# First f and decay rows issued by ScalarE, raw loads of three pairs queued ahead, first k rounded by GpSimd, first probabilities turned in float32

## The chip, the cores and the metric

The kernel runs on one core of one Trainium2 chip. The metric is the device time of one execution in microseconds (us). TensorE (PE in the profile, PEld for its weight loads), VectorE (DVE), ScalarE (ACT), GpSimd (POOL) and SyncE (SP, which here only issues DMAs) run side by side, each through its own queue in order.

## The reference

Causal attention with a decay, then a mixture of experts with one expert per token. Cut to what matters here:

```python
scores = scale * q @ k.T                       # 8 batches x 8 heads, 576 x 64
cum    = cumsum(log(clip(f, 1e-4, 1)), -1)     # f: one number per token and head
scores = where(causal, -1e9, scores + cum[..., :, None] - cum[..., None, :])
attn   = exp(scores - rowmax); attn /= attn.sum(-1) + 1e-9
x      = attn @ v                              # then the experts: gate, w1, relu, w2
```

## The kernel before

Heads go in pairs: 32 pairs n, each on 128 partitions with one head in 64 of them. The program is one stream over steps (n, i), i from 0 to 6, in `attention_all`. In step (n, i) the scores of pair n are made (`s_steps`), the probabilities of pair n-1 are turned (transposed) on TensorE (`t_steps`), and in i = 1 the product with v of pair n-2 is made (`av`, L540). Routing and the experts' work are mixed into the later pairs and follow them. At the end of each step `order.pin()` (L807) keeps what was traced on each engine in program order; all SP DMAs go through `sp_dma` (L215) in program order too.

**Scores.** A score tile is a sum of two products in float32r (`smm`, L408): the first of `qk1` (q rounded in 64 partitions, what rounding left in the other 64) with the rounded k, the second of `Q2s`/`K2s`, 68 partitions that hold the raw q and k's remainder in 64 partitions and, in rows 64 to 67, the decay: cumulated log f of queries and keys and constants. `Q2s` and `K2s` exist twice, so pair n+2 writes where pair n was read. Score tiles go to three PSUM buffers (`ps_s`); VectorE adds the mask and takes the row extreme (`s_red`, L420), ScalarE takes the exponential (`s_exp`, L426).

**Operands of a pair.** `load_pair` (L219) loads a pair's raw q (two halves h, 320 KB each) and k (288 KB each); raw buffers are for three pairs. For pair 0: `first_q` (L344, ScalarE rounds q, then copies raw q into `Q2s`), `first_k` (L352, ScalarE rounds k, head by head), `second_q` (L357) and `second_k` (L360), remainders on VectorE (`lo`, L329). For pair 1 the same in the steps of pair 0, with the copy into `Q2s` on GpSimd. From pair 2 on GpSimd does `q_parts` (L367) and `copies` (L376), and k is rounded by `k_first` (L372; ScalarE for pair 2, VectorE later).

**The start.** SP issues the load of f (L241), pair 0 and pair 1's q. VectorE clips f, ScalarE takes the log (two table loads around it), VectorE scans and splits it in two (L249 to L263). SP then issues the decay rows of pair 0 (`c_rows`, L391: five small DMAs from the tile `xT0w` into `Q2s`/`K2s`; j is the head), pair 1's k, pair 2's q, rows of pair 1, pair 2's k. In step (1, 0) follow the rows of pair 2, pair 3's four loads and `c_writes` (L717: the rows of all later pairs to DRAM, 608 KB), in (1, 2) pair 4's loads, in (2, 0) `load_c` for pair 3 (L383: rows back from DRAM). `load_v` loads pair n's v in step (n, 3). GpSimd makes constant rows, masks and identities at the start.

**Turning.** `turn` (L475) transposes a 128x128 block with the float32r identity, reading the probabilities under a float32r name (`c.words`; `c.values` is the same memory named float32). A pair has 25 such blocks. The copies out of PSUM are VectorE's for pair 0 (`e` in `t_steps`) and mostly ScalarE's later.

Of the kernel before, what the change touches and what calls it, by code (L numbers as in the profile page):

```python
# [19 lines left out]
P = 128  # L20
# [147 lines left out]
def setup_consts(c, tc):  # L168
    c.ident = c.const.tile([P, P], F32, name="ident")
    make_identity(tc.nc, c.ident)  # L170
    c.identr = c.const.tile([P, P], F32R, name="identr")
    tc.nc.gpsimd.tensor_copy(c.identr, c.ident)


def attention_all(c, tc, qkT, va, vb, f, wgd, x_dram, batch_done, more_consts, extra):
# [15 lines left out]
    with ExitStack() as st:  # L191
# [27 lines left out]
        def load_pair(n, parts=(0, 1)):  # L219
# [21 lines left out]
        sp_dma(fr, f)  # L241
        warm = c.const.tile([1, 1], F32, name="warm")
        V.memset(warm, 1.0)
        tc.keep_in_program_order(nc.scalar.activation(warm, warm, AF.Ln))
        load_pair(0)
        load_pair(1, (0,))
        V.memset(ones, 1.0)
        V.memset(cum[:, 512:], 0.0)
        V.tensor_scalar(fr, fr, 1.0e-4, 1.0, ALU.max, ALU.min)  # L249
        nc.scalar.activation(fr, fr, AF.Ln)  # L250

# [28 lines left out]


        mask = ap_.tile([P, 512], F32, name="mask")
        nc.gpsimd.memset(mask, 0.0)
        nc.gpsimd.affine_select(
            mask[:, 384:], mask[:, 384:], [[-1, P]], ALU.is_ge, NEG,
            base=0, channel_multiplier=1,
        )
        maskj = ap_.tile([P, JW], F32, name="maskj")
        nc.gpsimd.memset(maskj, 0.0)
        for j in range(2):  # L290
            mj = maskj[j * 64 : j * 64 + 64, JW - 64 :]
            nc.gpsimd.affine_select(
                mj, mj, [[-1, 64]], ALU.is_ge, NEG, base=0, channel_multiplier=1
            )
        setup_consts(c, tc)
        const_rows(1)


# [3 lines left out]
        def late_consts():  # L302
            nc.gpsimd.memset(wg, 0.0)
            nc.gpsimd.memset(gTs[1][:, S - 512 :], 0.0)
            for i in range(2):
                nc.gpsimd.memset(c.values[i, "J"][:, S:], 0.0)
            c.more = more_consts()
# [10 lines left out]
        for vb_t in vbs:  # L318
            nc.gpsimd.memset(vb_t[64:KB], 0.0)
# [22 lines left out]
        pin = tc.keep_in_program_order  # L342

        def first_q(n):  # L344
            qk1, raw, q2 = operands(n), raws[n], Q2s[n]
            pin(nc.scalar.copy(qk1[:, 0:QW], raw[:, 0:QW]))
            if n == 0:
                pin(nc.scalar.copy(q2[0:64], raw[0:64, 0:QW]))
            else:
                nc.gpsimd.tensor_copy(q2[0:64], raw[0:64, 0:QW])  # L350

        def first_k(n):  # L352
            qk1, raw = ops[n][0], raws[n]
            for c0, c1 in ((QW, QW + S), (QW + S, QW + 2 * S)):
                pin(nc.scalar.copy(qk1[:, c0:c1], raw[:, c0:c1]))  # L355

        def second_q(n):  # L357
            pin(lo(V, n, ops[n][0][64:128, 0:QW], 64, 0, QW))

        def second_k(n):  # L360
            k2 = ops[n][3]
            for j in range(2):
                lo(V, n, k2[0:64, j], 0, QW + j * S, QW + (j + 1) * S)
# [27 lines left out]
        def c_rows(n, j):  # L391
# [3 lines left out]
            if j == 0:  # L395
                sp_dma(k2c[:, 0, :], r[:, :, 0:S])
                sp_dma(q2c[:, 0:640], r)
            else:
                sp_dma(k2c[:, 1, 0:512], r[:, :, 0:512])
                sp_dma(k2c[:, 1, 512:], r[:, :, S:640])  # L400
                sp_dma(q2c[:, 640:], r)
# [6 lines left out]
        def smm(out, n, parts, k0, kw):  # L408

            q1, k1, q2, k2 = ops[n]  # L410
            i, last = 0, 2 * len(parts) - 1
            for ql, kl in ((q1, k1), (q2, k2)):
# [18 lines left out]

        def s_tiles(n, items):

            b, p = divmod(n, NPAIR)
            pb = psum(ps_s)
            o = 0
            for j, t in items:
                w = P * (t + 1)
                smm(pb[:, o : o + w], n, [(j, j * 640 + P * t)], 0, w)
# [35 lines left out]
        def turn(out, words):  # L475

            note(nc.tensor.transpose(out.bitcast(F32R), words, c.identr))  # L477

        def t_tiles(n, items, engs):
# [3 lines left out]
            for j, t in items:  # L483
                for k in range(t + 1):
                    turn(pt[:, o : o + P], region(c.words, n, j, t)[:, P * k : P * k + P])
# [11 lines left out]
        def t_one(n, eng):  # L497
            aT = aTs[n]
            pt = psum(ps_t)
            for j in range(2):  # L500
                for k in range(2):
                    o = P * (2 * j + k)
                    turn(pt[:, o : o + P], region(c.words, n, j, 1)[:, P * k : P * k + P])
# [5 lines left out]
        def t_joint(n, eng):  # L509
            aT, sc = aTs[n], region(c.words, n, 0, -1)  # L510
# [11 lines left out]
        def t_last(n, pt):  # L522

            turn(pt[0:KB], region(c.words, n, 0, -1)[:, 512 : 512 + KB])
# [155 lines left out]
        def s_steps(n):  # L680
# [3 lines left out]
                      [(0, 1), (1, 1)])  # L684
            r = [(lambda g=g: (s_begin(n) if n not in nms else None, s_tiles(n, g)),
# [1072 lines left out]
```

## Time and profile before

| what | value |
|---|---|
| median of 3 runs (lowest to highest) | 797.3 us (797.06 to 799.41) |
| profiled execution, its own time | 800.95 us |
| its span, first to last instruction | 799.2 us |
| busy: PE | 773.7 us (97%) |
| busy: ACT, DVE, POOL | 513.3, 579.9, 541.7 us |
| mean granted TensorE clock | 0.993 |
| DMA | 114.70 MB, 144 GB/s over the span |

A span's start is the first instruction; times in the rows count from there. The profiled execution took 3.65 us more than the median of the runs. The busy share of PE includes the time in which a matmul runs at the lower clock, so it doesn't show by itself where time can be won.

### The profile page before, as it was taken

Reading aid. Unit: us, or ns where it says so; the run is one execution under the profiler, and the core shown is the slowest. Engines: PE = TensorE matmul, PEld = TensorE weight load, DVE = VectorE, ACT = ScalarE, POOL = GpSimd, SP = SyncE. Lnnn points to the kernel's source line nnn. Section 1 sums busy time; section 2 is a strip of 40 time slices with the busy share of each in tenths; the row PEclk is TensorE's granted clock in tenths of the full one; section 3 lists DMA queues with packets and bytes.
Section 4 is the critical chain, followed back from the end, with each engine's and each line's share of the span. In section 5 each row is a group of like instructions: output and inputs, shape, how many; then the busy total and the mean of one; then the engine's idle time right before and its main releaser. Section 6 shows DMA issues by size and latency. Waiting matters only on the chain.

```text
span 799.2 us, 16185 instructions
## 1 busy us (share of the span) xinstructions
PE 773.7 (97%) x5496; PEld 673.7 (84%) x5496; DVE 579.9 (73%) x1654; ACT 513.3 (64%) x1278; POOL 541.7 (68%) x466
## 2 busy tenths in 40 slices
PE   4999999999999999999999999999999999999996
PEld 3878878787878888898988899898898898998985
DVE  7756989898989989856398848758477488486630
ACT  6868888888888888945355646455365465463521
POOL 6989889898989898762567657546556475475311
PEclk9989999999999999999999999999999999999999
DMA  7898787878787875523345352363343433523300
GB/s 184 215 198 184 170 199 172 195 172 201 166 201 165 198 173 149 189 99 99 115 141 162 106 173 76 106 200 103 122 136 107 153 93 106 169 68 111 106 27 31
DMA packets 66825, 114.70 MB, mean 144 GB/s; under 512 B 8295, under 2 KB 39015, under 8 KB 63412
## 3 DMA queue, kind: packets, MB, share of 16 engines
q1 hardware_dynamic: 59700, 93.71, 45.5%
q0 software_dynamic: 6400, 19.93, 7.6%
q8 instruction: 44, 0.72, 0.4%
q14 instruction: 41, 0.34, 0.1%
q10 hardware_dynamic: 640, 0.01, 0.0%
HBM read 94.05 MB, written 20.55 MB: 143 GB/s over the span
## 4 chain that ended last, share of the span: by engine, by line
PE 56%; POOL 26%; DVE 6%; issue 6%; DMA 3%; ACT 2%; SPq 0%; POOLq 0%; ACTq 0%; DVEq 0%
PE ps L1194 27%; PE ps L1393 18%; POOL qk L330 8%; POOL k L330 8%; POOL qk L369 3%; POOL q L379 3%; PE ps L1164 3%; PE ps L553 2%; POOL Rr L973 2%; PE ps L414 2%; DMA js<-jsum 2%; PE ps L477 1%; PE pr L1393 1%; PE ps L1349 1%; DVE sc L421 1%
## 5 line engine op out<-in xcount | busy, mean ns | idle before, releaser
L428 ACT ACTIVATE sc<-sc,nmx 128x512 f32<-128x512 f32 (+3 forms) x256 | 142.5, 558 | 13.3 <-DVE nmx L421 11.7
L421 DVE CUSTOM_DVE_ANT_0 sc<-ps,mask 128x512 f32<-128x512 f32 (+3 forms) x256 | 115.1, 484 | 33.6 <-PE ps L414 31.3
L414 PE MATMUL ps<-qk 128*128 128x288 f32 (+4 forms) x384 | 125.5, 358 | 12.6 <-ACT qk L355 10.0
L1194 PE MATMUL ps<-w_0w,hhw 128*128 128x512 f32 x280 | 112.9, 403 | 0.0
L414 PE MATMUL ps<-k,q 68*128 68x288 f32 (+4 forms) x384 | 108.2, 329 | 4.4 <-POOL qk L369 1.8
L1393 PE MATMUL ps<-X_0w,w1s 128*128 128x320 f32 x504 | 111.9, 309 | 0.0
L1194 PE MATMUL ps<-w_0w,hl 128*128 128x512 f32 x280 | 110.8, 396 | 0.0
L1194 PE MATMUL ps<-w_1w,hhw 128*128 128x512 f32 x280 | 110.3, 394 | 0.0
L1202 POOL DMA_INDIRECT out<-y,si_fast x37 | 37.4, 1011 | 98.2 <-ACT y L1201 89.7
L553 PE MATMUL ps<-aT,va_t 128*64 128x256 f32 (+3 forms) x896 | 96.0, 358 | 0.0
L473 ACT COPY aT<-ps 128x512 f32<-128x512 f32 (+1 forms) x156 | 82.6, 530 | 17.3 <-PE ps L477 17.1
L330 POOL TENSOR_TENSOR qk<-raw,qk 64x1280 fp32r<-64x1280 f32 x30 | 88.2, 2938 | 2.4
L330 POOL TENSOR_TENSOR k<-raw,qk 64x1152 fp32r<-64x1152 f32 x30 | 79.8, 2661 | 11.6 <-DVE qk L373 11.6
L414 PEld LDWEIGHTS ps<-qk 128*128 128x128 f32 x384 | 70.9, 197 | 16.7 <-ACT qk L355 10.0
L1393 PEld LDWEIGHTS ps<-X_0w,w1s 128*128 128x128 f32 x504 | 84.2, 188 | 0.2
L1201 ACT ACTIVATE y<-ps,g_fast 128x512 f32<-128x512 f32 x37 | 25.5, 689 | 88.0 <-PE ps L1194 65.8
L553 PEld LDWEIGHTS ps<-aT,va_t 128*64 128x64 f32 x896 | 59.5, 138 | 26.6 <-issue 1.6
L414 PEld LDWEIGHTS ps<-k,q 68*128 68x128 f32 x384 | 72.8, 199 | 8.0 <-POOL k L330 3.0
L1393 PE MATMUL ps<-X_1w,w1s 128*128 128x320 f32 x252 | 77.9, 309 | 0.0
L1435 POOL TENSOR_TENSOR u<-u,u 128x320 f32<-128x320 f32 x28 | 24.6, 879 | 61.5 <-DVE u L1433 61.4
L1194 PEld LDWEIGHTS ps<-w_0w,hl 128*128 128x128 f32 x280 | 52.4, 187 | 12.8
L1194 PEld LDWEIGHTS ps<-w_1w,hhw 128*128 128x128 f32 x280 | 52.8, 189 | 11.0
(238 smaller groups left out, 1893.0 us busy)
## 6 DMA issues: line engine op xcount, KB each, us to landing
raw<-in_qkT SPq DMA_DIRECT2D x52, 608.0 KB
w1r<-in_w SPq DMA_DIRECT2D x112, 128.0 KB
w<-in_w SPq DMA_DIRECT2D x28, 512.0 KB
va_t<-in_va SPq DMA_DIRECT2D x32, 256.0 KB
x_dram<-row SPq DMA_DIRECT2D x32, 256.0 KB
raw<-in_qkT SPq DMA_DIRECT2D x12, 320.0 KB
wraw<-in_w SPq DMA_DIRECT2D x7, 512.0 KB
raw<-in_qkT SPq DMA_DIRECT2D x12, 288.0 KB
```

The lines of the kernel that those rows point to most:

```text
L330: return eng.tensor_tensor(o, raws[n][p0 : p0 + 64, c0:c1], ops[n][0][p0 : p0 + 64, c0:c1].bitcast(F32), ALU.subtract,)
L369: nc.gpsimd.tensor_copy(qk1[:, 0:QW], raw[:, 0:QW])
L414: note(nc.tensor.matmul(out, ql[:, q0 : q0 + P], kl[:, j, k0 : k0 + kw], start=(i == 0), stop=(i == last),))
L421: V.tensor_tensor_reduce(dst[:, 0 : src.shape[1]], src, m, -0.125, init, ALU.add, ALU.min, nms[n][:, col : col + 1],)
L428: nc.scalar.activation(x, x, AF.Exp, bias=nms[n][:, col : col + 1], scale=-1.0, accum_out=acc)
L473: nc.scalar.copy(dst, src)
L553: c.last_av = note(nc.tensor.matmul(pv[j * HD : (j + 1) * HD, q0 - qa : qb - qa], l, r, start=(blk == 0), stop=(blk == nb - 1),))
L1194: c.note(nc.tensor.matmul(py, rows(hi_, ft), w[wi], start=(ft + k == 0), stop=(ft == FT - 1 and k == 2),))
L1201: nc.scalar.activation(y, py, AF.Copy, scale=g[:, s : s + 1])
L1202: nc.gpsimd.indirect_dma_start(out=self.out, out_offset=bass.IndirectOffsetOnAxis(ap=si[:, s : s + 1], axis=0), in_=y, in_offset=None, bou ...
L1393: self.nc.tensor.matmul(bank[:, 0:HN], w[:, wi, mat, kt], x[xi][:, kt, :], start=start and k == 0, stop=k == 5, skip_group_check=True,)
L1435: G.tensor_tensor(p5, u3, p5, ALU.add)
```

## The change

- f is loaded by a DMA that ScalarE issues, ahead of its first table load, and the five row DMAs of pair 0 are issued by ScalarE between the rounding of q for pair 0 and of q for pair 1.
- SP's raw loads: pair 0, pair 1's q and one half of its k ahead of the rows; behind them in SP's order the other half, pair 2's q, rows of pair 1 and pair 2's k mixed, and pair 3's q (before: in step (1, 0)). One added edge orders the other half of k behind the last row DMA in issue. Pair 3's k and pair 0's v stand in step (1, 0), the v load moved there from (0, 3).
- GpSimd instead of ScalarE copies pair 0's raw q and rounds its k; GpSimd instead of VectorE makes the remainder of pair 1's q. The half masks and the float32r identity come behind pair 0's k on GpSimd. Constant rows of pair 1, zeros of v, gate and joint tiles are set by VectorE instead of GpSimd.
- The first products of pair 0's first three score groups are issued ahead of their second ones (`s_ahead`).
- Pair 0's probabilities are turned from the float32 name with the float32 identity; of the copies of the turned tiles of pair 0, those of steps 1 and 3 go from VectorE to ScalarE. `second_k` of pair 1 is one step earlier, `first_k` too.

```diff
-def setup_consts(c, tc):
+def setup_consts(c, tc, pin):
     c.ident = c.const.tile([P, P], F32, name="ident")
...
     c.identr = c.const.tile([P, P], F32R, name="identr")
-    tc.nc.gpsimd.tensor_copy(c.identr, c.ident)
...
-        def load_pair(n, parts=(0, 1)):
+        def load_pair(n, parts=(0, 1), halves=(0, 1), behind=None):
...
-                for h in range(2):
+                for h in halves:
                     last = sp_dma(raw[h * HD : (h + 1) * HD, c0:c1], qkT[b, p, :, c0:c1])
+            if behind is not None:
+                tc.add_manual_dep(
+                    last.ins, behind.ins.name,
+                    mybir.DependencyInfo(
+                        mybir.DependencyClass.NoSync, mybir.DependencyReason.DATA
+                    ),
+                    reason="behind the rows",
+                )
...
-        sp_dma(fr, f)
+        pin = tc.keep_in_program_order
+        pin(nc.scalar.dma_start(fr, f))
...
         load_pair(0)
         load_pair(1, (0,))
+        load_pair(1, (1,), (0,))
...
+        pin(V.memset(ones, 1.0))
+        pin(V.memset(cum[:, 512:], 0.0))
+        const_rows(1, V, (0, 1))
+        pin(V.tensor_scalar(fr, fr, 1.0e-4, 1.0, ALU.max, ALU.min))
         nc.scalar.activation(fr, fr, AF.Ln)
+        const_rows(1, V, (2,))
...
+        def rest_of_masks():
+            pin(nc.gpsimd.memset(maskj, 0.0))
+            for j in range(2):
+                mj = maskj[j * 64 : j * 64 + 64, JW - 64 :]
+                pin(nc.gpsimd.affine_select(
+                    mj, mj, [[-1, 64]], ALU.is_ge, NEG, base=0, channel_multiplier=1
+                ))
+            pin(nc.gpsimd.tensor_copy(c.identr, c.ident))
...
         def late_consts():
-            nc.gpsimd.memset(wg, 0.0)
-            nc.gpsimd.memset(gTs[1][:, S - 512 :], 0.0)
+            for vb_t in vbs:
+                pin(V.memset(vb_t[64:KB], 0.0))
+            pin(V.memset(wg, 0.0))
...
             if n == 0:
-                pin(nc.scalar.copy(q2[0:64], raw[0:64, 0:QW]))
-            else:
-                nc.gpsimd.tensor_copy(q2[0:64], raw[0:64, 0:QW])
+                pin(nc.gpsimd.tensor_copy(q2[0:64], raw[0:64, 0:QW]))
...
-                pin(nc.scalar.copy(qk1[:, c0:c1], raw[:, c0:c1]))
+                pin((nc.scalar.copy if n else nc.gpsimd.tensor_copy)(
+                    qk1[:, c0:c1], raw[:, c0:c1]))

         def second_q(n):
-            pin(lo(V, n, ops[n][0][64:128, 0:QW], 64, 0, QW))
+            pin(lo(nc.gpsimd if n else V, n, ops[n][0][64:128, 0:QW], 64, 0, QW))
+            if n:
+                pin(nc.gpsimd.tensor_copy(ops[n][2][0:64], raws[n][0:64, 0:QW]))
...
+        def s_ahead(groups):
+
+            for items in groups:
+                (j, t), pb = items[0], psum(ps_s)
+                smm(pb[:, 0 : P * (t + 1)], 0, [(j, j * 640 + P * t)], 0, P * (t + 1), (0,))
+                ahead.append(pb)
...
         def turn(out, words):

-            note(nc.tensor.transpose(out.bitcast(F32R), words, c.identr))
+            if words.dtype == F32:
+                note(nc.tensor.transpose(out, words, c.ident))
+            else:
+                note(nc.tensor.transpose(out.bitcast(F32R), words, c.identr))
+
+        def tiles(n):
+
+            return c.words if n else c.values
...
+            e1 = "s"
...
-                lambda: t_tiles(n, [(1, 3)], e),
+                lambda: t_tiles(n, [(1, 3)], e1),
                 lambda: t_tiles(n, [(0, 2), (0, 0)], e + "v"),
-                lambda: t_tiles(n, [(1, 2), (1, 0)], e + "v"),
+                lambda: t_tiles(n, [(1, 2), (1, 0)], e1 + "v"),
...
-        first_q(0)
-        first_k(0)
-        second_q(0)
-        second_k(0)
-        c_rows(0, 0)
-        c_rows(0, 1)
-        load_pair(1, (1,))
-        load_pair(2, (0,))
-        c_rows(1, 0)
-        c_rows(1, 1)
-        load_pair(2, (1,))
...
+        first_q(0)
+        second_q(0)
+        for j in range(2):
+            rows = c_rows(0, j, lambda o, i: pin(nc.scalar.dma_start(o, i)))
+        first_k(0)
+        second_k(0)
+        rest_of_masks()
+        late_consts()
+        with tc.issue_after(rows.ins):
+            first = load_pair(1, (1,), (1,), rows)
+            load_pair(2, (0,))
+            c_rows(1, 0)
+            load_pair(2, (1,), (0,))
+            c_rows(1, 1)
+            load_pair(2, (1,), (1,))
+            load_pair(3, (0,))
...
                 if n == 0:
                     if i == 0:
                         first_q(1)
-                        late_consts()
+                        second_q(1)
                     elif i == 2:
-                        second_q(1)
-                    elif i == 3:
                         first_k(1)
-                    elif i == 5:
+                    elif i == 4:
                         second_k(1)
...
                         c_rows(2, 0)
                         c_rows(2, 1)
-                        load_pair(3)
+                        load_pair(3, (1,))
+                        load_v(0)
                         c_writes()
...
-                if i == 3 and n < NP:
+                if i == 3 and 0 < n < NP:
                     load_v(n)
```

## Rows read from the trace of the kernel before

**Rows 1.** The waits by engine and line, longest first, of the stretch 12 to 70 us (two of them): what waited for what, us in total, times, longest us.
```profile
POOL k L330 <- DVE qk L373: 1.9, 1, 1.9
...
PE ps L414 <- POOL qk L369: 1.8, 1, 1.8
```

**Rows 2.** The waits of TensorE from 70 to 320 us, all of them.
```profile
PE ps L414 <- DVE nmx L421: 2.4, 6, 0.4
PE ps L414 <- POOL k L330: 0.6, 4, 0.2
```

**Rows 3.** The timeline of TensorE from 39 to 58 us (start, us, what; idle time before it in brackets): pair 3's start with the product of pair 1 and v, then pair 4's start, which has the same work.
```profile
39.20 0.46 PE L414 MATMUL ps<-qk 128*128 128x512 f32 x1
41.43 0.76 PE L414 MATMUL ps<-k,q 68*128 68x512 f32 x1 [1.77 <-POOL qk L369]
...
48.86 0.44 PE L414 MATMUL ps<-qk 128*128 128x384 f32 x1
...
53.13 0.46 PE L414 MATMUL ps<-qk 128*128 128x512 f32 x1
53.43 0.40 PE L414 MATMUL ps<-k,q 68*128 68x512 f32 x1
53.66 0.46 PE L477 MATMUL ps<-identr,sc_03w 128*128 128x128 f32 x4
...
54.89 1.84 PE L553 MATMUL ps<-aT,va_t 128*64 128x256 f32 x16
...
57.76 0.44 PE L414 MATMUL ps<-qk 128*128 128x384 f32 x1
```

**Rows 4.** Stretches (from:to, length; busy us and instructions of PE, PEld, DVE, ACT, POOL; granted clock; DMA share; GB/s).
```profile
10.00:12.50 2.50, 0.92 (x2) 0.45 (x2) 1.52 (x2) 1.20 (x2) 2.31 (x5) 1.00 0.20 45
22.50:25.00 2.50, 2.50 (x14) 2.50 (x12) 2.25 (x9) 2.19 (x6) 2.44 (x2) 1.00 0.05 10
30.00:39.00 9.00, 9.00 (x79) 7.64 (x79) 5.82 (x23) 7.52 (x22) 8.71 (x10) 1.00 1.06 261
42.00:44.00 2.00, 2.00 (x11) 1.61 (x9) 1.02 (x3) 1.30 (x3) 2.00 (x1) 0.50 1.02 239
```

**Rows 5.** The timeline of SP from 23 to 35 us: pair 3's raw loads, the row writes to DRAM, pair 4's raw loads, v of pair 1, rows of pair 3 (the second of two).
```profile
23.69 2.43 SPq L217 DMA_DIRECT2D raw<-in_qkT  x4
26.17 1.32 SPq L217 DMA_DIRECT2D cq<-xT0w  x2
...
29.73 3.02 SPq L217 DMA_DIRECT2D raw<-in_qkT  x4
...
34.45 0.25 SPq L217 DMA_DIRECT2D k<-ck  x1
```

**Rows 6.** The timeline of GpSimd: the first of pair 2's and of pair 3's operands, the last of pair 3's and of pair 4's.
```profile
19.57 1.53 POOL L369 CAST qk<-raw 128x1280 fp32r<-128x1280 f32 x1 [6.38 <-DMA raw<-in_qkT]
...
29.10 1.25 POOL L369 CAST qk<-raw 128x1280 fp32r<-128x1280 f32 x1 [1.05 <-DMA raw<-in_qkT]
...
35.05 2.66 POOL L330 TENSOR_TENSOR k<-raw,qk 64x1152 fp32r<-64x1152 f32 x1
...
46.12 2.61 POOL L330 TENSOR_TENSOR k<-raw,qk 64x1152 fp32r<-64x1152 f32 x1
```

**Rows 7.** The timeline of the start on SP, VectorE and TensorE, up to the first two products of a score tile.
```profile
0.80 0.59 SPq L217 DMA_DIRECT2D aT<-in_f  x1
...
1.02 0.54 DVE L247 MEMSET aT<- 64x576 f32 x1
...
3.61 0.51 DVE L249 TENSOR_SCALAR aT<-aT 64x576 f32<-64x576 f32 x1 [1.81 <-DMA aT<-in_f]
...
8.30 0.75 SPq L217 DMA_DIRECT2D k<-xT0w  x1
...
12.37 0.77 PE L414 MATMUL ps<-k,q 68*128 68x512 f32 x1 [1.55 <-DMA q<-xT0w]
```

**Rows 8.** The timeline of VectorE and TensorE in pair 0 and of TensorE in pair 1.
```profile
14.76 1.49 DVE L330 TENSOR_TENSOR qk<-raw,qk 64x1280 fp32r<-64x1280 f32 x1
...
18.56 1.42 DVE L330 TENSOR_TENSOR k<-raw,qk 64x576 fp32r<-64x576 f32 x2
...
19.99 0.77 PE L414 MATMUL ps<-k,q 68*128 68x512 f32 x1 [0.17 <-DVE k L330]
...
20.55 0.67 PE L477 MATMUL ps<-identr,sc_03w 128*128 128x128 f32 x4
...
21.02 0.76 PE L414 MATMUL ps<-qk 128*128 128x512 f32 x1
...
29.74 0.76 PE L414 MATMUL ps<-qk 128*128 128x512 f32 x1
...
30.72 0.57 PE L477 MATMUL ps<-identr,sc_03w 128*128 128x128 f32 x4
```

**Rows 9.** The one other small DMA that ScalarE issues (L574): its issue and the GpSimd instruction that waits for it, and the DMA queues' packets, MB and share of the 16 engines in 57.9 to 60 us and in 62 to 64 us (q1 is SP's queue, q10 ScalarE's).
```profile
57.94 0.51 ACTq L574 DMA_DIRECT2D js<-jsum  x1
65.25 0.31 POOL L578 COPY ssum<-js 64x4 f32<-64x4 f32 x1 [0.94 <-DMA js<-jsum]
...
q1 hardware_dynamic: 64, 0.47, 102.4%
...
q10 hardware_dynamic: 78, 0.00, 2.5%
```

More of the change, by code (lines that the diff above doesn't have):

```diff
@@ L5 @@
 from concourse import mybir
-from concourse.masks import make_identity
 from concourse._compat import with_exitstack
@@ L240, in attention_all, with const_rows @@
         fr, ones, cum = cwork[:, 0:S], cwork[:, S : 2 * S], cwork[:, 2 * S :]
[L241 removed]
+        pin = tc.keep_in_program_order
+        pin(nc.scalar.dma_start(fr, f))
         warm = c.const.tile([1, 1], F32, name="warm")
[L243 to L244 removed]
+        pin(V.memset(warm, 1.0))
+        pin(nc.scalar.activation(warm, warm, AF.Ln))
         load_pair(0)
         load_pair(1, (0,))
[L247 to L249 removed]
+        load_pair(1, (1,), (0,))
+        NQ = 2
+        Q2s = [ap_.tile([68, QW], F32R, name=f"q2_{i}") for i in range(NQ)]
+        K2s = [ap_.tile([68, 2, S], F32R, name=f"k2_{i}") for i in range(NQ)]
+        def const_rows(i, eng, parts=(0, 1, 2)):
+            q2, k2 = Q2s[i], K2s[i]
+            if 0 in parts:
+                pin(eng.memset(q2[64:68].bitcast(F32), -8.0))
+                pin(eng.memset(q2[64:68, S:640].bitcast(F32), 0.0))
+                pin(eng.memset(q2[64:68, 1152:1216].bitcast(F32), 0.0))
+            for j in range(2):
+                if j + 1 in parts:
+                    pin(eng.memset(k2[64:68, j].bitcast(F32), 8.0))
+        pin(V.memset(ones, 1.0))
+        pin(V.memset(cum[:, 512:], 0.0))
+        const_rows(1, V, (0, 1))
+        pin(V.tensor_scalar(fr, fr, 1.0e-4, 1.0, ALU.max, ALU.min))
         nc.scalar.activation(fr, fr, AF.Ln)
+        const_rows(1, V, (2,))
         tc.keep_in_program_order(nc.scalar.activation(warm, fr[0:1, 0:1], AF.Exp))
@@ L389, in load_c, with c_rows @@
             )
-        def c_rows(n, j):
+        def c_rows(n, j, start=sp_dma):
             q2c, k2c = (t[n % NQ][r : r + 2].bitcast(F32) for t, r in ((Q2s, 64), (K2s, 66)))
@@ L406, in s_begin, with smm @@
             nms[n] = sm.tile([P, 12], F32, name="nmx", bufs=3)
-        def smm(out, n, parts, k0, kw):
+        def smm(out, n, parts, k0, kw, products=(0, 1)):
             q1, k1, q2, k2 = ops[n]
-            i, last = 0, 2 * len(parts) - 1
-            for ql, kl in ((q1, k1), (q2, k2)):
+            i, last = len(parts) * products[0], 2 * len(parts) - 1
+            for ql, kl in [((q1, k1), (q2, k2))[x] for x in products]:
                 for j, q0 in parts:
@@ L430, in s_exp @@
             )
+        ahead = []
+        def s_ahead(groups):
[3 more added lines that the diff above has]
+                ahead.append(pb)
         def s_tiles(n, items):
             b, p = divmod(n, NPAIR)
-            pb = psum(ps_s)
+            rest = ahead.pop(0) if ahead else None
+            pb = psum(ps_s) if rest is None else rest
             o = 0
@@ L438, in s_tiles @@
                 w = P * (t + 1)
-                smm(pb[:, o : o + w], n, [(j, j * 640 + P * t)], 0, w)
+                smm(pb[:, o : o + w], n, [(j, j * 640 + P * t)], 0, w,
+                    (0, 1) if rest is None or o else (1,))
                 o += w
@@ L484, in t_tiles @@
                 for k in range(t + 1):
-                    turn(pt[:, o : o + P], region(c.words, n, j, t)[:, P * k : P * k + P])
+                    turn(pt[:, o : o + P], region(tiles(n), n, j, t)[:, P * k : P * k + P])
                     o += P
@@ L502, in t_one @@
                     o = P * (2 * j + k)
-                    turn(pt[:, o : o + P], region(c.words, n, j, 1)[:, P * k : P * k + P])
+                    turn(pt[:, o : o + P], region(tiles(n), n, j, 1)[:, P * k : P * k + P])
             copy_on(
@@ L509, in t_joint @@
         def t_joint(n, eng):
-            aT, sc = aTs[n], region(c.words, n, 0, -1)
+            aT, sc = aTs[n], region(tiles(n), n, 0, -1)
             pt = psum(ps_t)
@@ L522, in t_last @@
         def t_last(n, pt):
-            turn(pt[0:KB], region(c.words, n, 0, -1)[:, 512 : 512 + KB])
+            turn(pt[0:KB], region(tiles(n), n, 0, -1)[:, 512 : 512 + KB])
             lasts[n] = pt
@@ L684, in s_steps @@
                       [(0, 1), (1, 1)])
+            if n == 0:
+                step(lambda: s_ahead(groups[:3]))
             r = [(lambda g=g: (s_begin(n) if n not in nms else None, s_tiles(n, g)),
@@ L723, in c_writes @@
             sp_dma(ck[:, :, 1, 512:], cwf[NPR:NH, :, S:640])
+        first_q(0)
+        second_q(0)
+        for j in range(2):
+            rows = c_rows(0, j, lambda o, i: pin(nc.scalar.dma_start(o, i)))
[11 more added lines that the diff above has]
+            load_pair(3, (0,))
         tasks, among, c.later, order = {}, {}, [], InOrder(tc)
```

49 lines of the change are left out of this document (17 added, 32 removed).

## The prediction

> **What bounds the kernel now.** First the waits of the pairs' stretch by engine, then all waits of TensorE after it: from 70 to 320 us it waits 3.0 us in all [rows 2], and by the page it is busy 97% of the span. So behind the start TensorE's queue is full, and the end moves by what TensorE loses or gains before. GpSimd is nearly as full, but does wait for others, 1.9 us before 70 us [rows 1], so it has some slack. The change edits nothing behind step (1, 0), except the ends of loads; I look for what TensorE loses up to there and in what follows from the loads.
>
> Three losses stand there. **The start**: score tile (0, 3) gets its second product only at 12.37, when the decay rows land [rows 7]. **Pair 1**: its first second product waits for VectorE's remainder of k until 19.99 [rows 8]. **Pair 3**: TensorE makes a first product at 39.20 and the second only at 41.43, 1.77 us idle [rows 1, 3]. The row names GpSimd's L369 for pair 4, but what the product needs from GpSimd, pair 3's k remainder, ended at 37.7 (35.05 + 2.66) [rows 6]. So I read it as another: the rows of pair 3 out of DRAM, the last of which SP issued at 34.45 behind pair 3's and pair 4's raw data, the row writes and a v, 1,216 + 608 + 1,216 + 288 = 3,328 KB; the DMA engines had been idle until 25 [rows 4, 5]. At 250 GB/s that is 13.3 us, 38.3; with the 2.2 us that f took from the end of its issue to its waiter (1.39 to 3.61 [rows 7]), 40.5, near 41.4 (at 235 GB/s it fits). [...]
>
> **Start, term by term.** f from ScalarE instead of SP: the same issue time, raw data starts 0.65 us earlier (0.80 instead of 1.45 [rows 7]). f then shares the engines with raw data; cost from 0 to 1.3 us (one raw half of 320 KB at 250 GB/s ahead of it); I take 0.3. VectorE's memsets of constant rows: 1,280 + 576 columns and two short ones at 0.54 us per 576 [rows 7] are 1.9 us, in an idle gap of 1.81 [rows 7], so 0.2 late; the last one lies beside ScalarE's log. Pair 0's k rounded and q copied by GpSimd lie ahead of 12.37, cover enough. The first products ahead save TensorE time in pair 0, but VectorE then paces that pair, so 0.
>
> The rows of pair 0 go from SP's queue to ScalarE's. The trace's other small DMA of ScalarE, 1 KB, was issued at 57.94 and landed at 65.25; while SP's queue was full, q10 moved no packet (57.9 to 60), and its 78 packets went in 62 to 64 [rows 9]. By this row ScalarE's rows wait for the raw data issued ahead of them, 2.29 MB instead of 2.00, 1.15 us more, less the 0.65 earlier start: 0.5 late. [...]
>
> So pair 0's rows come some 0.7 us late with the memsets (and f's 0.3). But VectorE loses 1.49 us of work between its first reduction and pair 1's k remainder, pair 1's q remainder, which goes to GpSimd [rows 8]; there it takes 2.9 us in what was a gap of 6.38 us before 19.57 [rows 6]. Pair 1's gate moves by 1.49 - 0.7 - 0.3 = **0.5 us earlier** (from 1.0 late, if f waits for a raw half too, to 1.5 early).
>
> **Loads.** Pair 2's and pair 3's q fill the DMA gaps around 10 to 12.5 and 22.5 to 25 (shares 0.20 and 0.05) [rows 4]. GpSimd's waits of 6.38 and 1.05 us [rows 6] end: pair 2 starts some 2.5 us earlier, then waits for ScalarE's k of pair 2; pair 3 starts about 2 us earlier. Behind the gap stand 3,328 - 640 + 288 = 2,976 KB ahead of pair 3's rows (v of pair 0 is moved there), 1.4 us less, and SP gets there 0.5 earlier: they land near 39.5. TensorE wants them at 39.5 (where it went idle) - 0.5 + what the turned tiles cost, so the stall goes, **1.8 us**, and with it the lower clock, **3.1 us**. The gain can't pass GpSimd's: its pair 4 operands end at 48.7 [rows 6], TensorE began pair 4 at 53.13 [rows 3], slack 4.4 us and the 2 above, so 6.4 us.
>
> **Float32 turns.** 25 of 128 columns, all in pair 1, where TensorE is at the lower level (four turns in 0.47 us, 20.55 to 21.02, against 0.30 in pair 4, 53.66 to 53.96) and without gaps [rows 3, 8]. No row shows a float32 turn. Below: nothing, 0.117 us each as now. Above: the only large float32 work is `av`, 32 matmuls with 3,200 columns, two heads in two halves of the array, 2.87 us (54.89 to 57.76 [rows 3]): 1.79 ns per column and half, against 0.52 for score products (two of 512 in 0.53 us, 53.13 to 53.66), 3.5 times; then 0.29 us more each, 7.3 us. I take the upper end, the row with this number type, for the work, but not all of it for the time: pair 1 (19.99 to 29.74, 9.75 us [rows 8]) becomes 17.05 us at the lower clock, and if the clock rises as long after its start as behind 41.43 (7.4 us), the remaining 9.65 take 4.8: 12.25 us, 2.5 more; pair 2, whose first us was at the lower clock before (until 30.7 [rows 8]), gains 0.5. **Cost 2.0 us**, range 0 to 7.3. The copies moved from VectorE to ScalarE cost nothing: both have room in a longer pair 1.
>
> **Sum.** 1.8 + 3.1 + 0.5 - 2.0 = 3.4 us less. The profiled execution took 800.95, so 797.55; it stands 3.65 above the median, so against the median of 797.3 this is **793.9 us**.
>
> **Rivals.**
> 1. *Float32 turns cost what they do now* (0.22): the same blocks, the same columns, nothing but the number type. Then 1.8 + 3.1 + 0.5 = 5.4, less some 0.3 of stall, as TensorE comes to pair 3 at 39.0 and the rows near 39.5: 792.2. [...]
> 2. *The edge holds nothing, the change doesn't do what it says* (0.15): an edge of issue order between two engines may hold nothing when it runs. Then SP puts the rest of pair 1's k and pair 2's q, 928 KB, ahead of the rows: 3.7 us later by [rows 9], less the 0.7 for which the j = 1 rows would have been late anyway. Pair 1's gate is 2.5 late instead of 0.5 early; 4.9 - 2.5 - 2.0 = 0.4: 796.9.
> 3. *The stall stays* (0.15): GpSimd was the releaser, as the row says, or the rows come as late; then TensorE meets the same wait at 41.4 whatever it won before, with the lower clock behind it: 797.3. Against it stands the k remainder's end at 37.7.
> 4. *The clock rises late*, the other side (0.12): place, pair 1. If it rises only in the `av` of step (2, 1), as it rose at 48 us in that of (3, 1), the turns cost the full 7.3, and pair 2's start another 3.1 ([rows 3], the same work at both levels): 4.9 + 0.5 - 7.3 - 3.1 = -5.0, so 802.3. It decides from the point where the clock is still low when the last turn is done. For it speaks that the clock before stayed low from 12.4 to 30.7 though TensorE had little idle time; against it, that float32 turns leave fewer gaps.
>
> **How the numbers follow.** The forecast has 0.36, its own range 791.5 to 795.5. About 0.3% (2.4 us) is what a measurement of this kernel can tell from no change, so faster is under 794.9. Forecast and rival 1 give 0.58, less what of the forecast's range lies above, plus a little of rival 2: 0.57 faster. Rivals 2 and 3 make 0.30 the same; rival 4, and a late f together with rival 2, 0.13 slower. The range is from 790.8 (rival 1 with a start 1.4 better) to 798.5 (rivals 2 and 3 with f late); rival 4 and some edges are left out.
>
> **What would show it.** In the changed profile: TensorE's second product of pair 0 near 13, pair 1's first second product near 19.5; pair 1 about 12 us long, its turns near 0.4 us each, then 0.2; GpSimd's L369 without waits for raw data; no stall ahead of pair 3's first second product, and a granted clock of 1.00 from 42 to 48. It would be wrong if the decay rows landed after 15, if pair 1 took 17 us, if the clock fell to 0.50 again around pair 3, or if TensorE waited behind 70 us for GpSimd by more than the 0.6 us of now.

## The result: 0.9% slower, and the profile after

| kernel | median us (lowest to highest) | ratio to before, 95% interval |
|---|---|---|
| before | 797.2 (797.01 to 799.41) | 1 |
| changed | 804.9 (803.57 to 806.62) | 1.0088 [1.0073, 1.0103] |

The profiled execution of the changed kernel took 804.82 us, its span 803.1. The start first: its timeline on ScalarE's queue, VectorE, ScalarE and TensorE (start, us, what; idle time before it).

```profile
0.80 0.60 ACTq L251 DMA_DIRECT2D aT<-in_f  x1
...
5.87 0.97 DVE L276 TENSOR_SCALAR aT<-aT 64x576 f32<-64x576 f32 x1 [1.88 <-DMA aT<-in_f]
...
8.98 1.24 ACT L361 CAST qk<-raw 128x1280 fp32r<-128x1280 f32 x1
...
11.50 1.19 ACTq L754 DMA_DIRECT2D k<-xT0w  x1
12.72 0.58 ACTq L754 DMA_DIRECT2D q<-xT0w  x1
...
14.66 0.57 ACTq L754 DMA_DIRECT2D q<-xT0w  x1
...
17.51 0.76 PE L430 MATMUL ps<-k,q 68*128 68x512 f32 x1 [2.56 <-DMA q<-xT0w]
19.29 1.08 PE L430 MATMUL ps<-k,q 68*128 68x512 f32 x2 [1.02 <-DMA q<-xT0w]
```

Against [rows 7], f reaches VectorE's clip 2.3 us later (3.61 to 5.87), the first row is issued 3.2 us later (8.30 to 11.50) and the first second product comes 5.1 us later (12.37 to 17.51): the rows need longer on their way, too. SP's raw transfers in this stretch, after the first seven, which it had issued by 5.3:

```profile
11.38 0.47 SPq L218 DMA_DIRECT2D raw<-in_qkT  x1
...
12.79 1.55 SPq L218 DMA_DIRECT2D raw<-in_qkT  x2
```

These three, 928 KB, are the half of pair 1's k and pair 2's q that the added edge should have kept behind the last row. The last row is issued at 14.66; SP issues them at 11.38, 12.79 and 13.88. The instructions and semaphore events of the trace say what SP waited for: the eighth raw transfer waits for the semaphore of the fifth, which landed at 11.37, and for no row. (In this trace the first sixteen DMAs of SP and ScalarE use eight semaphores, each twice. None of the second eight was issued before the first DMA on its semaphore had landed, and the three raw transfers were issued within 0.01 us of that: 11.38, 12.79 and 13.88 behind 11.37, 12.78 and 13.87.) So the edge held nothing when the kernel ran. By the same events the three transfers landed at 15.01, 17.19 and 18.81, and the five rows, issued at 11.50 to 14.66 between them, at 15.13, 17.37, 17.62, 18.98 and 19.16.

The same timeline further on, on GpSimd, VectorE and TensorE:

```profile
16.72 2.88 POOL L347 TENSOR_TENSOR qk<-raw,qk 64x1280 fp32r<-64x1280 f32 x1 [1.78 <-issue]
...
20.85 1.25 POOL L385 CAST qk<-raw 128x1280 fp32r<-128x1280 f32 x1
...
22.18 2.91 POOL L347 TENSOR_TENSOR qk<-raw,qk 64x1280 fp32r<-64x1280 f32 x1
...
22.49 4.93 DVE L347 TENSOR_TENSOR k<-raw,qk 64x576 fp32r<-64x576 f32 x2
...
25.15 1.66 POOL L395 CAST q<-raw 64x1280 fp32r<-64x1280 f32 x1
...
28.26 0.76 PE L430 MATMUL ps<-qk 128*128 128x512 f32 x1 [3.62 <-DVE nmx L437]
28.82 0.63 PE L430 MATMUL ps<-k,q 68*128 68x512 f32 x1
29.25 1.05 PE L505 MATMUL ps<-ident,sc 128*128 128x128 f32 x4
29.96 0.77 PE L430 MATMUL ps<-qk 128*128 128x512 f32 x1
...
34.60 0.66 PE L505 MATMUL ps<-ident,sc 128*128 128x128 f32 x4
35.02 0.36 PE L430 MATMUL ps<-qk 128*128 128x256 f32 x1
...
37.56 0.48 PE L430 MATMUL ps<-qk 128*128 128x512 f32 x1
...
46.48 0.47 PE L430 MATMUL ps<-qk 128*128 128x512 f32 x1
46.78 0.40 PE L430 MATMUL ps<-k,q 68*128 68x512 f32 x1
```

GpSimd makes pair 1's q remainder at 16.72; what it does from 20.85 on (L385, then L347 at 22.18 and the copy at 25.15) is pair 2's q. Beside that, VectorE's k remainder of pair 1 begins 3.9 us late (18.56 to 22.49) and takes 4.93 us instead of 1.42 [rows 8], 3.5 more; with what VectorE still has to do for pair 0 behind it, pair 1's second product comes 8.8 us late (19.99 to 28.82). Pair 1 is then quick (9.3 us), pair 3 has no stall (46.48 and 46.78), and the clock behind it is full, in the stretch 47 to 49 us (columns as in [rows 4]):

```profile
47.00:49.00 2.00, 2.00 (x19) 1.56 (x20) 1.85 (x8) 1.70 (x6) 1.87 (x6) 1.00 0.91 155
```

So the stall and the lower clock of [rows 3] are gone from this trace, but TensorE comes to pair 3 7.3 us later than there (39.20 to 46.48), and the kernel is slower.

### The profile page after: what moved, and what is told of

The parts are those of the page before. It is cut to its first block, busy times and chain, and to the rows that moved or that the text cites. A ratio compares the mean times of both kernels' runs of the same rounds, so it can differ in the third digit from the quotient of the medians.

```text
span 803.1 us, 16180 instructions
## 1 busy us (share of the span) xinstructions
PE 769.4 (96%) x5496; PEld 670.6 (84%) x5496; DVE 590.7 (74%) x1663; ACT 511.7 (64%) x1277; POOL 544.6 (68%) x460
## 4 chain that ended last, share of the span: by engine, by line
PE 52%; POOL 33%; issue 8%; DVE 3%; DMA 2%; ACT 1%; ACTq 0%; SPq 0%; POOLq 0%
PE ps L1236 25%; PE ps L1435 17%; POOL qk L347 11%; POOL k L347 10%; POOL qk L385 4%; POOL q L395 4%; PE ps L1206 2%; POOL Rr L1015 2%; PE ps L587 2%; PE pr L1435 1%; PE ps L1391 1%; PE ps L430 1%; PE ps L507 1%; DMA raw<-in_qkT 1%; DVE w1s L1340 1%
## 5 line engine op out<-in xcount | busy, mean ns | idle before, releaser
L430 PE MATMUL ps<-qk 128*128 128x288 f32 (+4 forms) x384 | 123.7, 354 | 19.4 <-DVE qk L347 13.4
L347 POOL TENSOR_TENSOR qk<-raw,qk 64x1280 fp32r<-64x1280 f32 x31 | 91.9, 2963 | 4.2 <-issue 1.8
L587 PE MATMUL ps<-aT,va_t 128*64 128x256 f32 (+3 forms) x896 | 94.0, 353 | 0.0
L347 POOL TENSOR_TENSOR k<-raw,qk 64x1152 fp32r<-64x1152 f32 x30 | 79.8, 2660 | 16.1 <-DVE qk L389 8.4
L430 PEld LDWEIGHTS ps<-k,q 68*128 68x128 f32 x384 | 71.6, 196 | 10.1 <-POOL k L347 5.5
```

The lines of the kernel that those rows point to most:

```text
L347: return eng.tensor_tensor(o, raws[n][p0 : p0 + 64, c0:c1], ops[n][0][p0 : p0 + 64, c0:c1].bitcast(F32), ALU.subtract,)
L430: note(nc.tensor.matmul(out, ql[:, q0 : q0 + P], kl[:, j, k0 : k0 + kw], start=(i == 0), stop=(i == last),))
L587: c.last_av = note(nc.tensor.matmul(pv[j * HD : (j + 1) * HD, q0 - qa : qb - qa], l, r, start=(blk == 0), stop=(blk == nb - 1),))
```

## Experiments

Times are medians, with the ratio to the kernel before run beside it on the same chip.

**1. The kernel before again**, unchanged.

> The kernel before, unchanged. Theory C (the profiled execution of before was not the usual one): the 1.8 us stall ahead of pair 3's second product and the 3.1 us of lower clock behind it are missing in this trace, the granted clock is above 0.993 and the profiled execution takes about 797 instead of 800.95. Rival: the stall is in every execution, and the trace shows it again with a profiled time near 801. Median 797.2 by both.

798.3 us. Its profiled execution (798.77) has no stall at pair 3; TensorE's timeline:

```profile
30.65 0.76 PE L414 MATMUL ps<-qk 128*128 128x512 f32 x1
...
40.73 0.47 PE L414 MATMUL ps<-qk 128*128 128x512 f32 x1
41.04 0.40 PE L414 MATMUL ps<-k,q 68*128 68x512 f32 x1
...
49.62 0.46 PE L414 MATMUL ps<-qk 128*128 128x512 f32 x1
```

TensorE comes to pair 3 1.5 us later than in [rows 3] and meets the rows there; pair 4 begins at 49.62 instead of 53.13. So the stall and the slow stretch behind it, 4.9 us, belong to the execution that stood 3.65 us above the median and not to every execution; how many of the others have them isn't shown.

**2. f, then the rows too, back on SP; pair 1's q remainder back on VectorE.**

```diff
-        pin(nc.scalar.dma_start(fr, f))                       # e_f_sp and e_f_rows_sp
+        sp_dma(fr, f)
-            rows = c_rows(0, j, lambda o, i: pin(nc.scalar.dma_start(o, i)))   # e_f_rows_sp
+            rows = c_rows(0, j)
-            pin(lo(nc.gpsimd if n else V, n, ...                # e_q1_v alone
+            pin(lo(V, n, ...
```

> The changed kernel with f loaded by SP ahead of the raw data again. Theory A (f on ScalarE's queue landed at 5.87 instead of 3.61 and held everything behind the log on ScalarE): f near 3.6, q of pair 0 rounded from 7 instead of 9, rows issued from 9 instead of 11.5, pair 1's first product about 2.5 us earlier (near 25.8), 2 to 3 us less in the end (802). Theory B (the loss is VectorE's slow k remainder of pair 1 beside GpSimd): the start is earlier, but the remainder still takes some 5 us; less than 1 us in the end (804).

801.4 us, 1.0051 [1.0030, 1.0073]: theory A. Rows issued from 9.49, SP's last three raw transfers between them again (10.84, 12.19, 13.39), pair 1's first product at 24.82, though the k remainder still took 4.73.

> The changed kernel with f and the rows of pair 0 on SP's queue again (the raw loads behind the rows now wait in SP's order). Theory A: the rows land 3.2 us after issue instead of 4.8 (12.72 to 17.51), pair 0's second product near 13.5, and 3 to 4.5 us less in the end than the changed kernel (801). Theory B: under 1 us less (804).

797.8 us, 1.0001 [0.9989, 1.0012]: the whole loss is gone. Rows issued from 9.48, second products from 13.83, pair 1 at 20.33. On SP's queue the rows come ahead of the last three raw transfers (from 12.79) by program order alone, so this run changes the queue and the order together; experiment 4 tells them apart.

> The changed kernel with the remainder of pair 1's q on VectorE again. Theory B (VectorE's k remainder of pair 1 took 4.93 us instead of 1.42 because GpSimd works at the same time): the two instructions take 0.75 us each again, pair 1's first product comes at 25 instead of 28.3, 3 us less in the end (802). Theory A: the start stays as late as it is, VectorE has 1.5 us more to do, and the time stays at 805 or is 1 us worse.

802.4 us, 1.0063 [1.0040, 1.0086]; the k remainder took 2.16 us, since GpSimd's work on pair 2 begins 2 us earlier (18.86 instead of 20.85) and is nearly done. GpSimd's remainder of pair 1 costs some 2 us, and only because all is late: in e_f_rows_sp GpSimd still makes it, at 13.99, and VectorE's k remainder then takes 1.92.

**3. Only the rows back on SP; f alone on ScalarE's queue in the kernel before; f late on SP.**

```diff
-            rows = c_rows(0, j, lambda o, i: pin(nc.scalar.dma_start(o, i)))   # e_rows_sp
+            rows = c_rows(0, j)
-        sp_dma(fr, f)                                           # before: e_before_f_act
+        tc.keep_in_program_order(nc.scalar.dma_start(fr, f))
         load_pair(0)                                            # e_f_late, on e_f_rows_sp
+        sp_dma(fr, f)
```

> The changed kernel with only the first pair's rows back on SyncE's queue; f stays on ScalarE's. Theory A (f and the rows each cost what they cost alone): 804.9 less 3.6 (what the rows gave when f was on SyncE) is 801.3 us; the q remainder still begins near 11.4 and the rows are issued near 11.5, landing by 15.5. Theory B (with f late the rows' queue doesn't matter): 804 to 805 us. Theory C (the rows are all of the loss): 798 us.

797.8 us, 1.0001 [0.9988, 1.0013]. Theory C; but in its profile f, on ScalarE's queue, reached the clip at 4.02, not at 5.75 to 5.93 as in the five other profiles with f there, so this run alone doesn't say that a late f is free. There f landed at 3.64, ahead of pair 0's first raw half (5.18); in the changed kernel at 5.85, behind it (5.23).

> The kernel before with f alone begun on ScalarE's queue. The prediction took 0.3 us for it, at most 1.3. Theory A (f's packets share the engines with the raw data, landing 2.3 us later, and the q rounding of pair 0 stands behind the log on ScalarE): clip near 5.9 instead of 3.6, first product 1 to 2.5 us later, and the time 1 to 3.5 us longer, unless TensorE's later arrival at pair 3 takes part of it back. Theory B (nothing waits for f): 798 us.

799.2 us, 1.0012 [0.9997, 1.0026]. The clip came at 5.93 and pair 1's second product at 22.34 instead of 20.11, but pair 3 only at 41.22 instead of 40.73: of 2.2 us about 1 is left, with an interval from nothing to 2.

> The changed kernel with the rows and f on SyncE's queue, f behind pair 0's four raw transfers, so that it surely lands late (near 5.9 us instead of 4.0). Theory A (a late f moves the whole start): rows issued near 11.4 instead of 9.5, second product at 15.7 instead of 13.8, pair 1 at 22 instead of 20.3, and 799 to 800 us. Theory B (the 2 us at the start are taken up by the wait at pair 3, which TensorE then reaches later): 797.5 to 798 us, as with f in time.

807.3 us, 1.0121 [1.0103, 1.0139]; a miss of both. Behind four raw transfers f reached VectorE at 9.47, not 5.9; the k remainders of both pairs fell beside GpSimd's work and took 5.05 and 5.20 us, and pair 1 began at 30.33.

**4. Why the rows are slow on ScalarE's queue.** The raw data behind the last row held until it has landed (e_hold: the edge now makes SP wait for the row's semaphore), and the rows alone on ScalarE's queue in the kernel before (e_before_rows_act: `c_rows` given `nc.scalar.dma_start`, the raw data behind it under `tc.issue_after(rows.ins)`, which held nothing either).

```diff
-                        mybir.DependencyClass.NoSync, mybir.DependencyReason.DATA   # e_hold
+                        mybir.DependencyClass.Sync, mybir.DependencyReason.DATA
```

> The changed kernel, rows still on ScalarE's queue, but SyncE sends the raw data behind them only when the last row has landed. Theory A (the rows are late because raw data is sent beside them): the second products of pair 0 come within 3.5 us of the rows' issue, so 16 and 16.5 or so instead of 17.5 and 19.3; what is won there may be lost again on pair 2's raw data, which starts 1 to 3 us later. Theory B (ScalarE's queue is slow for them whatever stands beside): second products at 17.5 and 19.3 as before, and a time above 805 us since the raw data is later too.

800.1 us, 1.0025 [1.0014, 1.0035], 0.6% less than the changed kernel by one word. Its timeline:

```profile
12.54 0.58 ACTq L754 DMA_DIRECT2D q<-xT0w  x1
...
14.37 0.56 ACTq L754 DMA_DIRECT2D q<-xT0w  x1
14.55 0.63 PE L430 MATMUL ps<-k,q 68*128 68x512 f32 x1
16.23 1.08 PE L430 MATMUL ps<-k,q 68*128 68x512 f32 x2 [1.05 <-DMA q<-xT0w]
...
20.58 1.42 DVE L347 TENSOR_TENSOR k<-raw,qk 64x576 fp32r<-64x576 f32 x2 [1.06 <-ACT qk L368]
...
22.83 0.77 PE L430 MATMUL ps<-qk 128*128 128x512 f32 x1 [1.25 <-ACT sc L444]
```

The last row landed at 16.10 and SP issued the eighth raw transfer at 16.11. The same DMA on the same queue takes at most 2.0 us (12.54 to 14.55), with the seventh raw transfer in at 13.76, where it took 4.8 (12.72 to 17.51) with the ninth issued beside it (12.79) and in at 17.19. So the queue isn't slow by itself; the order of issue makes the rows late, and with it 5 us of the loss. The queues from 14 to 16 us (packets, MB, share of the engines), first of the changed kernel, then of e_hold:

```profile
q1 hardware_dynamic: 99, 0.40, 76.8%
q10 hardware_dynamic: 4, 0.00, 0.9%
```

```profile
q10 hardware_dynamic: 12, 0.01, 2.0%
```

And with GpSimd idle (20.65 to 22.89) the k remainder takes 1.42 us again. What is left of the loss, some 2 us, fits the late f and the later raw data; it wasn't taken apart.

> The kernel before, with the first pair's rows alone begun on ScalarE's queue, at their place in its order, and the raw data issued behind the last of them as in the changed kernel. Theory A (the rows share the engines with the raw data that SyncE then sends at once): second product of pair 0 at 14.5 to 16 instead of 12.7; 2 to 4 us longer, 800 to 802 us. Theory B (the rows matter only where f is late and GpSimd has the first k): 798 us. The prediction's term (rows 0.5 us later): 798.5 us.

804.1 us, 1.0073 [1.0053, 1.0092]: moving the rows alone makes most of the loss, more than any theory said. Its timeline:

```profile
9.56 1.20 ACTq L710 DMA_DIRECT2D k<-xT0w  x1
...
10.80 0.59 ACTq L710 DMA_DIRECT2D q<-xT0w  x1
11.43 2.51 ACTq L710 DMA_DIRECT2D k<-xT0w  x2
17.51 0.56 ACTq L710 DMA_DIRECT2D q<-xT0w  x1
...
18.13 0.77 PE L414 MATMUL ps<-k,q 68*128 68x512 f32 x1 [7.16 <-DMA q<-xT0w]
```

The rows no longer stand in SP's order, and SP sent all ten raw transfers by 9.86, ahead of them, not behind the last row as the expectation had it. The last raw transfer landed at 17.72, and the row of 5 KB issued at 10.80 reached TensorE at 18.13, 7.3 us, as long as js [rows 9]. ScalarE itself stood 3.6 us (13.94 to 17.51) before it issued the last row. By the semaphore events it stood for the first row (issued 9.56, landed 17.43), whose semaphore the last row uses again; a limit of the queue isn't shown by it.

**5. The number type of the turns.** In the changed kernel `tiles(n)` returns `c.words` always (e_f32r); in the kernel before it gets the changed kernel's `turn` and `tiles` (e_before_f32).

> The changed kernel with the first pair's 25 tiles turned as rounded words again, as before the change; nothing else differs. Theory A (a float32 turn simply costs 0.06 us more at the lower clock, four in 0.71 instead of 0.47 us): 25 x 0.06 = 1.5 us back, 803.4 us. Theory B (the heavier float32 turns also bring the full clock sooner: pair 1 took 9.3 us with the rise 6.5 us behind its first product, and 10.5 us in the kernel before): the first product of pair 2 comes no earlier or 0.5 to 1.2 us later against that of pair 1, 805 to 806 us. Forecast of the prediction (turns at up to 0.29 us each over, 2.0 us in all): 802.9 us.

804.5 us, 1.0086 [1.0069, 1.0103]: no different from the changed kernel. Pair 1 took 10.0 us (28.11 to 38.16) instead of 9.3.

> The kernel before with the first pair's 25 tiles turned in float32; nothing else differs. Theory A (0.06 us more for each turn, clock rising when it did): 1.5 us slower, 798.9 against 797.4. Theory B (clock up sooner): pair 1 takes 8.7 to 9.5 us instead of 10.5, pair 2 begins at 29 to 29.8 instead of 30.65; unless pair 3 then waits for its rows, 796 to 796.6. The prediction's middle (2.0 us more): 799.4.

800.1 us, 1.0026 [1.0016, 1.0035]; the size was A's or the prediction's, the cause neither's. TensorE:

```profile
20.08 0.76 PE L414 MATMUL ps<-k,q 68*128 68x512 f32 x1 [0.34 <-DMA q<-xT0w]
...
27.89 0.48 PE L414 MATMUL ps<-qk 128*128 128x512 f32 x1
...
37.14 0.47 PE L414 MATMUL ps<-qk 128*128 128x512 f32 x1 [0.17 <-DVE nmx L421]
41.75 0.77 PE L414 MATMUL ps<-k,q 68*128 68x512 f32 x1 [4.14 <-DMA k<-ck]
```

Pair 1 to pair 2 takes 7.8 us instead of 10.5 (20.11 to 30.65): a gain. But TensorE then comes to pair 3 3.6 us sooner, stands 4.14 us for the rows out of DRAM, now named by the trace's line itself, and falls to the lower clock (granted 0.58 from 40 to 45 us, 0.74 from 45 to 50).

**6. Where a gain at the start goes.** Pair 3's rows read in step (1, 6), ahead of the k half of pair 4's raw data: on e_f_rows_sp (e_c3) and on e_before_f32 (e_before_f32_c3). On e_c3, GpSimd's first two blocks of routing constants, 2.45 us between pair 3's and pair 4's operands, go elsewhere: to the start, free in order (e_c3_more) or behind pair 0's q (e_pin), or into two idle gaps in pairs 0 and 1 (e_gaps).

```diff
+                    if i == 6 and n == 1:
+                        load_c(3)
+                        load_pair(4, (1,))
...
-                    load_pair(n + 3)
+                    load_pair(n + 3, (0,) if n == 1 else (0, 1))
```

> The changed kernel with f and the first pair's rows on SyncE's queue, and SyncE's order changed for pair 3: its rows are read behind pair 1's last joint product and ahead of the k half of pair 4's raw data, not behind all of it. Theory A (the 1.80 us that pair 3's second product waits at 38.4, and the lower clock until 50, come from rows that land late): second product within 0.5 us behind the first, near 38.3; pair 4 begins near 47.3 instead of 50.48; then it waits for GpSimd's k remainder of pair 4, about 1.5 us; 796.0 us. Theory B (pair 3 waits for GpSimd, whose k remainder ended at 37.76 and whose constants ran until 40.24): the second product stays at 40.2, 797.8 us.

797.1 us, 0.9991 [0.9982, 1.0000]: the second product at 38.26 and a wait of 1.50 at pair 4, as theory A has it, but 1.1 us above its time.

> The kernel before with the first pair's tiles turned in float32, and pair 3's rows read ahead of the k half of pair 4's raw data. Theory A (float32 turns are a gain of 2.7 us at pair 1, lost again only because pair 3's rows then land 4.1 us too late and the clock falls): pair 2 near 27.9, pair 3's second product within 0.5 us behind its first at 37.1, pair 4 near 46; then GpSimd's k remainder of pair 4 holds it 1 to 2 us; 795.5 to 796.5 us. Theory B (the turns themselves cost 2 us): 799.5 us or more.

797.8 us, 1.0000 [0.9988, 1.0012]. Pair 3's second product 0.56 us behind its first, pair 4's held 1.44 us by GpSimd. So float32 turns together with early rows cost nothing; the kernel before with the early rows alone wasn't run, so what each is worth isn't shown.

> As the kernel with pair 3's rows ahead, and GpSimd's first two blocks of routing constants (2.45 us between 37.7 and 40.2, ahead of pair 4's operands) put into its idle 2.3 us ahead of pair 0's k. Theory A (GpSimd sets the begin of pair 4's second products): no wait for GpSimd at pairs 4 and 5, 794.5 us. Theory B (GpSimd's constants at the start hold VectorE's q remainder or delay pair 0's k by over 0.5 us): pair 0's second product 0.5 to 1.5 us later than 13.83, 795.5 to 796.5 us. Theory C (another engine sets pairs 4 and 5): as the kernel without it.

796.7 us, 0.9978 [0.9969, 0.9987], faster than both kernels. Pairs 3 to 5 follow at 8.9 us without a wait; pair 1 was 2.1 us late (22.47), as its k remainder took 4.01 us beside GpSimd's.

> The kernel with f, the first pair's rows and pair 3's rows moved on SyncE's queue, and GpSimd's two blocks of routing constants (1.35 and 1.1 us) put where GpSimd was idle: 1.13 us ahead of pair 2's q (18.2) and 1.61 us ahead of pair 2's k remainder (24.9), no longer 37.7 to 40.2. Theory A (those 2.45 us are what pair 4's second product waits for, 1.50 us at 46.85): pair 3 begins near 38, pair 4's second product within 0.3 us of the first, pair 6 near 64.7 instead of 67.26; 794.5 to 795 us. Theory B (GpSimd beside VectorE's k remainder of pair 1 slows it again, as in the kernel with the constants at the start, where it took 4.01 us): pair 1 begins at 21 to 22.5, 796 to 796.7 us.

799.7 us, 1.0013 [0.9997, 1.0030]. A wait of 1.40 us at 54.7, then the lower clock (granted 0.57, 0.50, 0.50 and 0.73 in the four stretches of 2 us from 58 to 66).

> The kernel with f, the first pair's rows and pair 3's rows moved on SyncE's queue, GpSimd's two blocks of routing constants put behind the rounding of pair 0's second q and ahead of pair 0's k (idle there 2.0 to 2.3 us). Theory A (GpSimd's constants were what held pair 4 by 1.50 us, and the start is untouched): pair 1 near 20.5, pair 3 near 38.1 and pair 4 near 47.0 without waits over 0.5 us, pair 6 near 65; 794.5 to 795.5 us. Theory B (TensorE then only meets the next late transfer, as with the constants in the later gaps, which took 799.7 us with a wait of 1.4 us at 54.7 and the lower clock behind it): 797 to 800 us.

796.5 us, 0.9988 [0.9979, 0.9997]. Pair 1 at 21.15, pair 4 at 47.69 without a wait, but pair 5 only at 57.81, 10.1 us later.

TensorE of e_f_rows_sp, then of e_c3, shows how one late thing takes the place of the other:

```profile
28.98 0.47 PE L430 MATMUL ps<-qk 128*128 128x512 f32 x1
...
40.25 0.47 PE L430 MATMUL ps<-k,q 68*128 68x512 f32 x1 [1.80 <-POOL trib L893]
...
50.48 0.46 PE L430 MATMUL ps<-qk 128*128 128x512 f32 x1
```

```profile
37.95 0.47 PE L430 MATMUL ps<-qk 128*128 128x512 f32 x1
38.26 0.40 PE L430 MATMUL ps<-k,q 68*128 68x512 f32 x1
...
46.85 0.46 PE L430 MATMUL ps<-qk 128*128 128x512 f32 x1
48.81 0.50 PE L430 MATMUL ps<-k,q 68*128 68x512 f32 x1 [1.50 <-POOL k L347]
...
58.30 0.47 PE L430 MATMUL ps<-qk 128*128 128x512 f32 x1
```

The first reaches pair 2 1.7 us ahead of experiment 1's kernel and has lost it by pair 4. In the second the wait at 38.4 is gone by moving a DMA alone, though the row names GpSimd's constants: the releaser was the rows, as the prediction read the same row in [rows 3].

## Why the prediction was wrong

- **"Against the median of 797.3 this is 793.9."** This step failed first, by 4.9 us: the stall and the clock were subtracted from the median, as if every execution had them. The 3.1 us are the same work in [rows 3] at both paces, 7.43 us (41.43 to 48.86) with a granted clock of 0.50 from 42 to 44 us [rows 4] against 4.33 (53.43 to 57.76). Experiment 1 has neither. Without them its own terms leave 0.5 us won and 2.0 lost, so 798.8 us. That the profiled execution stood 3.65 us above the median should have been read as a sign.
- **"0.5 late" for the rows.** Failed, by the most: the first second product came 5.1 us late, 3.2 of them because the rows were issued late. The reading of js held: here too the rows came in behind raw data issued ahead of them or beside them, and a row of e_before_rows_act took 7.3 us behind ten raw transfers. Wrong was what stood ahead. The term counts 2.29 MB and takes it that the added edge keeps 928 KB behind the last row, but SP issued them at 11.38 to 13.88, ahead of and among the rows, and each row landed within 0.5 us behind a raw transfer that was issued ahead of it or beside it. This is the condition of rival 2, "the edge holds nothing", at a chance of 0.15. With an edge that does hold (e_hold) the first second product comes 3.0 us earlier, pair 1 5.4 us, and the time is 0.6% less. Packets of both queues moved side by side (99 of q1 and 4 of q10 from 14 to 16 us), but no row came early by it.
- **f, "I take 0.3", bound 1.3.** Mis-sized: 2.3 us at the clip. (VectorE's memsets, put at 0.2, would alone have made it 0.4: with f on SP the changed kernel clips at 4.01, in e_f_sp.) ScalarE's order carries it on, since the rounding of q stands behind the log (8.98; 6.98 before). Alone it cost about 1 us (e_before_f_act, interval 0 to 2), with the rows on ScalarE some 3 (0.88% to 0.51%).
- **GpSimd's q remainder "in what was a gap".** The gap was there, but the remainder in it pushed GpSimd's work on pair 2 back, and the late rows moved VectorE's k remainder beside that work: 4.93 us instead of 1.42, some 2 us of the loss (e_q1_v). The first of its two subtractions ended at 25.70, 0.61 us behind the end of GpSimd's subtraction (22.18 + 2.91 = 25.09), the second at 27.42, 0.61 us behind the end of GpSimd's copy (25.15 + 1.66 = 26.81): about the length of one alone, as if each had stood until then; what would make it stand isn't shown. In e_hold, where GpSimd was idle, the two took 1.42.
- **Turns, "cost 2.0 us".** Mis-sized: four take 0.71 us at the slower pace (29.25 to 29.96) instead of 0.47, so 0.06 us each, 1.5 at most, and the faster pace came within pair 1 (from 35.02), which took 9.3 us and not 12.25. Between e_f32r and the changed kernel there is no difference in time. Rival 1 was nearly right in size, the reference to `av` wrong.
- **Rivals 2 to 4.** Rival 2's condition held, as said; its 3.7 us for the rows is near the 3.0 of e_hold, but its 796.9 has the 4.9 us subtracted too, and leaves out f and the k remainder. Rival 3: no stall at pair 3, as TensorE came late; where it came early (e_f_rows_sp, 37.98), the wait was there again, 1.80 us. Rival 4: the faster pace came within pair 1, not at the `av` of step (2, 1). "Wrong if the decay rows landed after 15" came true: the first at 15.13, the last at 19.16.
- **Loads.** Half right: no gap on GpSimd ahead of pair 3's operands and pair 3 without a stall, but GpSimd began pair 2's at 20.85, not 2.5 us ahead of 19.57. It was worth nothing where TensorE came to pair 3 5.8 us later than in experiment 1.

## What to carry to other kernels

Look at how far the profiled execution stands from the median before you subtract a loss that it shows; a second profile of the same kernel is the cheapest test. When you take a DMA off the queue that carries the bulk data, check in the trace when the bulk is issued: here the edge of issue order alone held nothing (928 KB issued at 11.38 to 13.88, the last row at 14.66), while a wait on the row's semaphore (e_hold, 800.1 us) or the order of one queue (e_f_rows_sp, 797.8 us) held the bulk back. And a gain at the start counted here only as far as the next thing that ran dry had slack for it: first the rows (a wait of 4.14 us in e_before_f32), then GpSimd (1.50 us in e_c3). The granted clock fell behind the first wait (0.58 from 40 to 45 us) and stayed at 1.00 behind the second (45 to 60 us).

## What the hardware showed

- A DMA of 5 KB on ScalarE's queue took 2.0 us to its waiter with the raw data ahead of it in at 13.76 (e_hold), 4.8 us with a raw transfer of 320 KB issued 0.07 us behind it (changed kernel), 7.3 us behind ten raw transfers (e_before_rows_act). Why it comes in with the other queue's data, though packets of both move side by side, is open.
- Two VectorE subtractions of 64x576 float32 took 1.42 us with GpSimd idle and 4.0 to 5.2 us beside GpSimd's subtractions, copies and casts (five times in four profiles).
- f on ScalarE's queue reached VectorE at 5.75 to 5.93 us in five profiles and at 4.02 in one; what decides this is open.
- With float32 turns pair 1 took 7.8 and 8.6 us on the kernel before (e_before_f32, e_before_f32_c3), with rounded words 9.75 and 10.5 us (the first profile, e_before). In pair 1 of the changed kernel the products of 512 columns follow one another at the slower pace (0.56 us from one to the next, 28.26 to 28.82, against 0.30 at 46.48) though the row of granted clock says 1.00 there: at the start the pace has to be read from durations.
